# Tile 0 as up 0, up 1, down 0, down 1 with the weights loaded in that order, mixing-weight transposes earlier, batch 1 a group sooner

## Chip, core and metric

The kernel runs on one core of one Trainium2 chip. The metric is device time in microseconds (us) of the whole kernel. A comparison is made of runs on the same chip in the same rounds.

## The reference, cut to what matters

```python
# q, k, v: 8 batches, 8 heads, 576 positions, 64 dims; 4608 = 8 * 576 tokens
scores = scale * q @ k.T                      # per batch and head
ret    = (scores * decay_mask) @ v            # gamma_h ** (i - j) for i >= j, else 0
x      = ret as [4608 tokens, 512]
p      = domain_probs / (domain_probs.sum(-1) + 1e-9)
for e in range(4):                            # w1[e]: 512 x 1024, w2[e]: 1024 x 512
    out += p[:, e] * (relu(x @ w1[e]) @ w2[e])
```

The attention of a batch has to be ready before the expert layers can use its 576 tokens. The expert layers work on nine tiles of 512 tokens.

## The kernel before

TensorE runs the expert layers nearly without a break. The attention of the next batch is threaded between their groups of matmuls. A stage "up e" is 8 groups of 4 matmuls (0.86 us each); a stage "down e" is 4 groups of 8 matmuls (1.73 us each). `plan` says behind which group a piece of attention is issued, so `at(20, ...)` is a place in TensorE's order. 576 is not a multiple of 128: each batch has a remainder of 64 tokens, which is loaded, cast and transposed apart (`load_rem`, `cast_rem`, `Trem`; `Srem` makes its scores and `Orem` its output). Names in the profile: `ph` and `po` are the results of an up and a down group, `ptr` the transposed remainder, `sr` its scores, `s` the scores of other chunks, `qrb`, `krb`, `vrb` the cast remainder and `xT` the attention output that the expert layers read. A load "lands" when it is complete.

```python
def load_rem(b, gate=None):                 # raw_kr, raw_qr, raw_vr on the SP queue
    for n, src in SRC:
        ...
        i = nc.sync.dma_start(out=state[b][n + "r"], in_=src[b, :, SM:S, :].rearrange("h p d -> p h d"))
        if gate is not None and n == "k":
            after(i, gate)                  # SP waits here until the DMA `gate` has landed
...
def moe(nt, lead=0):                        # one tile; every yield ends a group
    ...
    for e in range(E):
        ...                                 # up e: 8 groups, then down e: 4 groups
...
w20 = load_w2(0)                            # weights: POOL queue, in this order
late_constants()
for e in range(1, E):
    load_w1(e)
    load_w2(e)
load_rem(0, w20)                            # the gate: w2 of expert 0
load_alloc(1)
load_chunk(1, 0)
load_chunk(1, 1)
...
if nt == 0:
    at(1, mixing_weights)
    at(3, lambda: a0.cast_rem(nc.gpsimd))   # POOL: krb, qrb, vrb
    at(20, a0.Trem)                         # TensorE: ptr <- qrb, krb
    at(22, a0.Srem, a0.Srem_mask)
    at(24, a0.Orem)
    ...                                     # begin1 at 25: casts of batch 1
elif nt + 1 < B:
    ...
    at(19 if nt == 1 else 17, lambda: state["A"].S([0, 1]))   # scores of the next batch,
                                            # from DMA transposes into qkT
```

Of the kernel before, what the change touches and what calls it, by code (L numbers as in the profile page):

```python
# [9 lines left out]
FP32 = mybir.dt.float32  # L10
BF16 = mybir.dt.bfloat16
# [9 lines left out]
def kernel(  # L21
# [10 lines left out]
    nc = tc.nc  # L32
    B, H, S, D = q.shape
    N, E = moe_domain_probs.shape
    _, Dm, F = moe_w1.shape
# [8 lines left out]
    NFC = F // 128  # L44
    NT = 512
# [108 lines left out]
                   allow_small_or_imprecise_dtypes=True)  # L154
    ident = const.tile([128, 128], BF16)
    make_identity(nc, ident)

    tri2 = const.tile([128, 2, 128], BF16)
    nc.gpsimd.memset(tri2, 1.0)
# [1 line left out]
        nc.gpsimd.affine_select(out=tri2[j:j + 64], in_=tri2[j:j + 64], compare_op=mybir.AluOpType.is_ge,  # L161
                                fill=0.0, base=0, channel_multiplier=-2, pattern=[[-1, 2], [1, 128]])
    tri = const.tile([128, 128], BF16)
    identf = const.tile([NTT, NTT], FP32)


    trir = const.tile([128, R], BF16)
# [1 line left out]
    def late_constants():  # L169
        nc.gpsimd.memset(tri, 1.0)  # L170
        nc.gpsimd.memset(trir, 1.0)
        for j in (0, 64):
            nc.gpsimd.affine_select(out=trir[j:j + 64], in_=trir[j:j + 64], compare_op=mybir.AluOpType.is_ge,
                                    fill=0.0, base=0, channel_multiplier=-1, pattern=[[1, R]])
        nc.gpsimd.affine_select(out=tri, in_=tri, compare_op=mybir.AluOpType.is_ge, fill=0.0,
                                base=0, channel_multiplier=-1, pattern=[[1, 128]])
        nc.gpsimd.tensor_copy(identf, ident[:NTT, :NTT])

    lgp = const.tile([128, NP], FP32)
    for p in range(NP):  # L180
# [19 lines left out]
    probs = const.tile([128, E, NTT], FP32)  # L200
    psm = const.tile([128, NTT], FP32)

    def mixing_weights():
        pp = ps_at.tile([128, E, NTT], FP32, tag="at", name="pp")
        for e in range(E):
            nc.tensor.transpose(pp[:, e, :], probs_raw[:, :, e], identf)
        nc.vector.tensor_copy(probs, pp)
        nc.vector.tensor_reduce(psm, probs[:, :, :].rearrange("p e t -> p t e"),
                                axis=mybir.AxisListType.X, op=ADD)
        nc.vector.tensor_scalar_add(psm, psm, 1e-9)  # L210
        nc.vector.reciprocal(psm, psm)
        nc.vector.tensor_tensor(probs, probs, psm[:, :].unsqueeze(1).to_broadcast([128, E, NTT]), op=MULT)
# [293 lines left out]
                                        gq[:, 2 * u:2 * u + 2, ts], op=MULT)  # L506


    def moe(nt, lead=0):
        n0 = nt * NT  # L510

        def up(ph, e, fc, ts):
            for dc in range(NDC):
                nc.tensor.matmul(ph[:, ts], lhsT=w1_sb[e][:, dc, fc * 128:(fc + 1) * 128],  # L514
                                 rhs=xT[:, dc, n0 + ts.start:n0 + ts.stop], start=(dc == 0), stop=(dc == NDC - 1))

        acc = [apool.tile([128, Dm], FP32, tag="acc", name="acc") for _ in range(NSUB)]
        for e in range(E):
            hT = hpool.tile([128, NFC, NT], BF16, tag="hT")
            for fc in range(NFC):  # L520
                if e == 0 and fc < lead:
                    if fc == 0:
                        early = [ps_mm.tile([128, NT], FP32, tag="mm", name="ph") for _ in range(lead)]
                        for x in range(lead):
                            up(early[x], e, x, slice(0, NT // 2))
                            if x != 1:
                                yield
                    ph = early[fc]
                    up(ph, e, fc, slice(NT // 2, NT))
                else:  # L530
                    ph = ps_mm.tile([128, NT], FP32, tag="mm", name="ph")
                    up(ph, e, fc, slice(0, NT))
                nc.scalar.activation(hT[:, fc, :], ph, Relu)  # L533
                yield
            for ns in range(NSUB):
                t = nt * NSUB + ns
                pe = probs[:, e, t:t + 1]
                last = t == NTT - 1 and e == E - 1
                w = Dm // 2 if last else Dm
                for d in range(0, Dm, w):  # L540
                    po = ps_mm.tile([128, w], FP32, tag="mm", name="po")
                    for fc in range(NFC):
                        nc.tensor.matmul(po, lhsT=hT[:, fc, ns * 128:(ns + 1) * 128],  # L543
                                         rhs=w2_sb[e][:, fc, d:d + w], start=(fc == 0), stop=(fc == NFC - 1))
                    a = acc[ns][:, d:d + w]
                    if e == 0:
                        nc.scalar.activation(a, po, Copy, scale=pe)  # L547
                    else:
                        nc.vector.scalar_tensor_tensor(a, po, pe, a, op0=MULT, op1=ADD)  # L549
                    if e == E - 1:  # L550
                        eng = nc.scalar if last and d // w % 2 else nc.sync
                        eng.dma_start(out=out[n0 + ns * 128:n0 + (ns + 1) * 128, d:d + w], in_=a)
                yield


    a0 = AttP(0)
    UNITS = [(hf, u) for hf in range(2) for u in range(2)]

    tiles = [moe(nt, lead=3 if nt < 2 else 0) for nt in range(n_nt)]
    tile0 = tiles[0]  # L560
    warm(8)
    for n, eng in (("k", nc.gpsimd), ("q", nc.scalar), ("v", nc.gpsimd)):
# [1 line left out]
    for x, (hf, u) in enumerate(UNITS):  # L564
        a0.T(hf, u, nc.scalar)
        if x < 2:
            load_gq((2 + x,))
        if x == 0:
            warm(4)
        else:  # L570
            a0.O(*UNITS[x - 1])
        if x < 3:
            a0.cast("k", *UNITS[x + 1], nc.gpsimd)
            a0.cast("q", *UNITS[x + 1], nc.gpsimd)
            if x:
                load_w1(0, x - 1)
            a0.cast("v", *UNITS[x + 1], nc.gpsimd)
        a0.S(hf, u)
        if x == 0:
            warm(2)  # L580
        a0.kv(hf, u)
    next(tile0)
    a0.O(*UNITS[3])
    next(tile0)
    w20 = load_w2(0)
    late_constants()
    for e in range(1, E):
        load_w1(e)
        load_w2(e)
    load_rem(0, w20)  # L590
# [5 lines left out]
    for nt in range(n_nt):  # L596
        plan = {}

        def at(g, *fs):
            plan.setdefault(g, []).extend(fs)  # L600

        if nt == 0:
            at(1, mixing_weights)
            at(3, lambda: a0.cast_rem(nc.gpsimd))
            at(20, a0.Trem)
            at(22, a0.Srem, a0.Srem_mask)
            at(24, a0.Orem)
            def begin1():
                A = state["a1"] = Att(1)
                for c in range(NCH):  # L610
                    for n in "kqv":
                        A.cast(n, c, nc.gpsimd)
                    if c == 0:
                        load_chunk(1, 2)
                        load_chunk(1, 3)
                load_rem(1)
                load(2)

            at(25, begin1)
            for c, g in enumerate((40, 42, 44, 46)):  # L620
                at(g, lambda c=c: state["a1"].Tc(c))
                if c < 3:
                    at(g + 1, lambda c=c: state["a1"].Sc(c))
                if c > 0:
                    at(g + 1, lambda c=c: state["a1"].Oc(c - 1))
                at(g + 1, lambda c=c: state["a1"].kv(c))
        elif nt + 1 < B:
            if nt == 1:
                a1 = state["a1"]
                at(0, lambda: a1.cast_rem(nc.gpsimd))  # L630
                at(2, a1.Trem)
                at(4, a1.Srem, a1.Srem_mask)
                at(6, a1.Orem)
            def begin(b=nt + 1):
                A = state["A"] = Att(b)
                for c in range(NCH):
                    for n in "kqv":
                        A.cast(n, c, nc.gpsimd)
                A.cast_rem(nc.gpsimd)
                for c in range(NCH + 1):  # L640
                    A.dmaT(c)
                if b + 1 < B:
                    load(b + 1)

            at(7 if nt == 1 else 0, begin)
            at(19 if nt == 1 else 17, lambda: state["A"].S([0, 1]))
            at(24, lambda: state["A"].Srem(), lambda: state["A"].O_values([0, 1]),
               lambda: state["A"].kv_all(), lambda: state["A"].kv_sum(), lambda: state["A"].Srem_mask())
            at(28, lambda: state["A"].O_states([0, 1]))
            at(30, lambda: state["A"].S([2, 3]))  # L650
            at(34, lambda: state["A"].O_values([2, 3], rem=True), lambda: state["A"].O_states([2, 3], rem=True))
        for g, _ in enumerate(tiles[nt]):
            for f in plan.get(g, ()):
                f()
        if nt == 0:
            state["a1"].Sc(3)
            next(tiles[1])
            next(tiles[1])
            state["a1"].Oc(3)


# [28 lines left out]
```

## Time and profile before

| | before |
|---|---|
| median time | 560.77 us (3 runs, before the change was run) |
| TensorE busy | 545.6 of 559.2 us |
| TensorE waits for w2 of expert 0 | 1.74 us, ends at 27.99 |
| gate of the remainder loads opens | 27.96 |
| cast qrb starts / transposes ptr start | 40.99 / 43.64 |

The page of the kernel before, its first parts (busy time and share of the span; granted TensorE clock in tenths per fortieth of the span):

```profile
PE 545.6 (98%) x3469; PEld 262.5 (47%) x3530; DVE 165.7 (30%) x283; ACT 217.0 (39%) x371; POOL 109.8 (20%) x182
PEclk9999999999999999999999999999999999999999
```

TensorE is the bound, at a mean granted clock of 1.000. Only its idle time can be won. The waits of TensorE in the kernel before, one of 0.5 us left out (total us, times, longest us):

```profile
PE pt L437 <- POOL qm L427: 2.3, 3, 1.0
PE po L543 <- DMA wt_492<-in_moe_w_dram: 1.7, 1, 1.7
PE warm_out L140 <- DVE warm_in L135: 1.3, 1, 1.3
PE ph L514 <- DVE xT L329: 0.8, 1, 0.8
...
PE ph L514 <- issue: 0.2, 1, 0.2
```

`wt_492` is w2 of expert 0. About 7 us of idle time in all, of which the change aims at the second, fourth and last line. The weights landed in the order in which they were issued: w2 of expert 0 at 27.95, then w1 and w2 of expert 1 at about 33.0 and 39.6 and w1 of expert 2 at about 45.3 (start of the issue plus time to landing). The SP queue's own waits show the gate:

```profile
SPq L115 <- DMA wt_492<-in_moe_w_dram: 17.0, 1, 17.0
```

TensorE's timeline around the remainder transposes (start, duration, what), and POOL's casts of the remainder:

```profile
41.82 1.89 PE L543 MATMUL po<-wt_502,hT 128*128 128x512 bf16 x8
43.64 0.29 PE L261 MATMUL ptr<-ident,qrb 64*128 64x64 bf16 x4
43.77 0.28 PE L261 MATMUL ptr<-ident,krb 64*128 64x64 bf16 x4
43.98 3.63 PE L543 MATMUL po<-wt_502,hT 128*128 128x512 bf16 x15
47.53 0.31 PE L336 MATMUL sr<-qkT 64*64 64x64 bf16 x8
```

```profile
36.57 1.04 POOL L240 TENSOR_TENSOR krb<-raw_kr,gk 64x512 bf16<-64x512 f32 x1 [13.16 <-DMA raw_kr<-in_k_dram]
40.99 0.60 POOL L243 CAST qrb<-raw_qr 64x512 bf16<-64x512 f32 x1 [3.38 <-DMA raw_qr<-in_q_dram]
```

The cast qrb ends at 41.59 and TensorE asks for it at 43.64: a margin of 2.0 us. The loads of kr and qr took 8.5 and 12.2 us from issue to landing, where the median of all batches is 5.4 and 4.5, because the weight queue was busy. In the half microsecond from 36.0 (weights in 2 KB rows) and in the one from 40.0 (4 KB rows), the two queues moved (packets, MB, share of 16 engines; q0 carries the weights, q1 the SP loads):

```profile
q0 software_dynamic: 78, 0.08, 93.5%
q1 hardware_dynamic: 78, 0.02, 29.9%
```

```profile
q0 software_dynamic: 46, 0.09, 98.9%
q1 hardware_dynamic: 47, 0.01, 18.0%
```

Equal packet counts, so the remainder, in packets of 256 bytes, gets a fifth of the bytes or less. (A weight row of 2 KB is cast to half its size on the way; the trace counts the 1 KB that is written: 0.08 MB in 78 packets.) This fits the round-robin between queue rows of the Trainium skill, "DMA: Bandwidth & Descriptors", section "Queues, rings and completion order". The trace agrees in the equal shares; how many rows an engine takes in one turn it does not show.

### The profile page before, as it was taken

Reading aid. Unit: us, or ns where it says so; the run is one execution under the profiler, and the core shown is the slowest. Engines: PE = TensorE matmul, PEld = TensorE weight load, DVE = VectorE, ACT = ScalarE, POOL = GpSimd, SP = SyncE. Lnnn points to the kernel's source line nnn. Section 1 sums busy time; section 2 is a strip of 40 time slices with the busy share of each in tenths; the row PEclk is TensorE's granted clock in tenths of the full one; section 3 lists DMA queues with packets and bytes.
Section 4 is the critical chain, followed back from the end, with each engine's and each line's share of the span. In section 5 each row is a group of like instructions: output and inputs, shape, how many; then the busy total and the mean of one; then the engine's idle time right before and its main releaser. Section 6 shows DMA issues by size and latency. Waiting matters only on the chain.

```text
span 559.2 us, 8453 instructions
## 1 busy us (share of the span) xinstructions
PE 545.6 (98%) x3469; PEld 262.5 (47%) x3530; DVE 165.7 (30%) x283; ACT 217.0 (39%) x371; POOL 109.8 (20%) x182
## 2 busy tenths in 40 slices
PE   7899999999999999999999999999999999999997
PEld 4544455454445444444445444544444444444443
DVE  5402262253214520462035212542046202220222
ACT  6442344433353235323433334323532353335332
POOL 7611247026001520044002600250010000000000
PEclk9999999999999999999999999999999999999999
DMA  9999999591369025910594058803300100010001
GB/s 232 176 203 200 209 206 231 104 213 15 104 131 180 1 84 89 217 28 38 109 179 92 0 123 157 135 1 98 63 2 1 73 3 0 1 76 0 1 0 75
DMA packets 148277, 53.83 MB, mean 96 GB/s; under 512 B 130668, under 2 KB 142188, under 8 KB 148240
## 3 DMA queue, kind: packets, MB, share of 16 engines
q1 hardware_dynamic: 141296, 44.79, 39.2%
q0 software_dynamic: 6800, 8.39, 8.8%
q8 instruction: 27, 0.44, 0.4%
q10 hardware_dynamic: 144, 0.13, 0.1%
q14 instruction: 10, 0.08, 0.1%
HBM read 45.16 MB, written 9.44 MB: 98 GB/s over the span
## 4 chain that ended last, share of the span: by engine, by line
PE 94%; DMA 3%; POOL 1%; issue 1%; SPq 1%; DVE 0%
PE po L543 44%; PE ph L514 43%; DMA wt_492<-in_moe_w_dram 2%; PE o L351 1%; DMA raw_k<-in_k_dram 1%; PE o L365 1%; SPq L85 1%; POOL km L423 0%; PE sr L336 0%; PE orem L358 0%; PE ptc L297 0%; POOL wt_269 L125 0%; PE kvb L389 0%; PE kva L389 0%; PE oc L322 0%
## 5 line engine op out<-in xcount | busy, mean ns | idle before, releaser
L533 ACT ACTIVATE hT<-ph 128x512 bf16<-128x512 f32 x288 | 171.6, 597 | 274.6 <-PE ph L514 274.6
L543 PEld LDWEIGHTS <-hT 128*128 128x128 bf16 x1160 | 112.5, 98 | 134.6 <-DMA wt_492<-in_moe_w_dram 2.2
L549 DVE SCALAR_TENSOR_TENSOR acc<-po,probs,acc 128x512 f32<-128x512 f32 (+1 forms) x109 | 81.3, 746 | 234.6 <-PE po L543 226.8
L514 PE MATMUL ph<-xT,wt_504 128*128 128x512 bf16 x280 | 66.3, 379 | 0.5
L514 PE MATMUL ph<-xT,wt_269 128*128 128x512 bf16 (+1 forms) x303 | 64.2, 362 | 1.4 <-DVE xT L329 0.8
L543 PE MATMUL po<-wt_492,hT 128*128 128x512 bf16 x286 | 63.4, 379 | 1.8 <-DMA wt_492<-in_moe_w_dram 1.7
L543 PE MATMUL po<-wt_506,hT 128*128 128x512 bf16 x273 | 63.8, 379 | 0.8
L514 PE MATMUL ph<-xT,wt_500 128*128 128x512 bf16 x280 | 64.1, 379 | 0.5
L543 PE MATMUL po<-wt_510,hT 128*128 128x512 bf16 (+1 forms) x287 | 63.4, 373 | 0.5
L514 PE MATMUL ph<-xT,wt_508 128*128 128x512 bf16 x286 | 63.7, 379 | 0.2 <-issue 0.2
L543 PE MATMUL po<-wt_502,hT 128*128 128x512 bf16 x280 | 63.4, 379 | 0.4
L403 POOL CAST sbd<-ksum 64x256 bf16<-64x256 f32 x36 | 14.4, 399 | 221.2 <-DVE ksum L408 197.6
L514 PEld LDWEIGHTS <-wt_269 128*128 128x128 bf16 x312 | 30.0, 98 | 32.1 <-issue 0.9
L514 PEld LDWEIGHTS <-wt_508 128*128 128x128 bf16 x288 | 28.0, 98 | 33.3
L514 PEld LDWEIGHTS <-wt_500 128*128 128x128 bf16 x288 | 27.7, 98 | 33.4
L514 PEld LDWEIGHTS <-wt_504 128*128 128x128 bf16 x288 | 26.9, 98 | 30.3
L547 ACT ACTIVATE acc<-po,probs 128x512 f32<-128x512 f32 x36 | 24.7, 687 | 40.1 <-PE po L543 39.1
L235 POOL TENSOR_TENSOR km<-raw_k,gk 128x512 bf16<-128x512 f32 x28 | 29.2, 1043 | 13.9 <-DMA raw_k<-in_k_dram 9.5
L237 POOL CAST vm<-raw_v 128x512 bf16<-128x512 f32 x28 | 17.3, 616 | 41.8 <-PE o L351 34.9
L237 POOL CAST qm<-raw_q 128x512 bf16<-128x512 f32 x28 | 17.1, 611 | 7.4 <-DMA raw_q<-in_q_dram 7.2
L374 DVE TENSOR_TENSOR xT<-o,gq 128x512 bf16<-128x512 f32 x24 | 15.5, 686 | 7.6 <-PE o L365 7.6
L240 POOL TENSOR_TENSOR krb<-raw_kr,gk 64x512 bf16<-64x512 f32 x8 | 8.3, 1037 | 13.8 <-DMA raw_kr<-in_k_dram 13.2
(231 smaller groups left out, 238.7 us busy)
## 6 DMA issues: line engine op xcount, KB each, us to landing
out_dram<-acc SPq DMA_DIRECT2D x35, 256.0 KB, 2.0
raw_k<-in_k_dram SPq DMA_DIRECT2D x32, 256.0 KB, 5.0
raw_q<-in_q_dram SPq DMA_DIRECT2D x32, 256.0 KB, 5.1
raw_v<-in_v_dram SPq DMA_DIRECT2D x32, 256.0 KB, 5.2
wt_269<-in_moe_w_dram POOLq DMA_DIRECT2D x2, 512.0 KB, 5.6
wt_492<-in_moe_w_dram POOLq DMA_DIRECT2D x1, 1024.0 KB, 11.7
wt_500<-in_moe_w_dram POOLq DMA_DIRECT2D x1, 1024.0 KB, 14.5
wt_502<-in_moe_w_dram POOLq DMA_DIRECT2D x1, 1024.0 KB, 20.4
```

What stands on the lines that cost most here:

```text
L85: nc.sync.dma_start(out=pairs_of(state[b][n, hf])[:, h], in_=src[b, h, 256 * hf:256 * hf + 256, :].rearrange("h (p j) d -> p h (j d)", j=2))
L235: eng.tensor_tensor(o, i, gk[:, c, :].unsqueeze(2).to_broadcast([128, H, D]), op=MULT)
L237: eng.tensor_copy(o, i)
L240: eng.tensor_tensor(self.r["k"], self.t["kr"], gk[:R, NCH, :].unsqueeze(2).to_broadcast([R, H, D]), op=MULT)
L351: nc.tensor.matmul(o[64 * j:64 * j + 64, c * C:(c + 1) * C], lhsT=self.m["v"][:, c, 2 * p + j, :], rhs=self.sT[p][:, j, c, :], start=(c == ...
L374: nc.vector.tensor_tensor(xT[:, p, b * S:b * S + SM], o, gq[:, p, 0:SM], op=MULT)
L403: eng.tensor_copy(sbd[r, n, :, r], src[r])
L514: nc.tensor.matmul(ph[:, ts], lhsT=w1_sb[e][:, dc, fc * 128:(fc + 1) * 128], rhs=xT[:, dc, n0 + ts.start:n0 + ts.stop], start=(dc == 0), s ...
L533: nc.scalar.activation(hT[:, fc, :], ph, Relu)
L543: nc.tensor.matmul(po, lhsT=hT[:, fc, ns * 128:(ns + 1) * 128], rhs=w2_sb[e][:, fc, d:d + w], start=(fc == 0), stop=(fc == NFC - 1))
L547: nc.scalar.activation(a, po, Copy, scale=pe)
L549: nc.vector.scalar_tensor_tensor(a, po, pe, a, op0=MULT, op1=ADD)
```

## The change

The intent: put two up stages ahead of the first down stage, so that w2 of expert 0 is needed one stage (6.9 us) later and its wait goes; fill another wait with the mixing-weight transposes; and have batch 1 ready a group sooner, so that tile 1 does not wait for xT.

```diff
+        first = [ups(0), ups(1), downs(0), downs(1)] if nt == 0 else [ups(0), downs(0), ups(1), downs(1)]
+        for stage in first + [g for e in range(2, E) for g in (ups(e), downs(e))]:
+            yield from stage
...
-    tiles = [moe(nt, lead=3 if nt < 2 else 0) for nt in range(n_nt)]
+    tiles = [moe(0, lead=3, pause=True), moe(1, lead=2, cut=3 * NT // 4)] + [moe(nt) for nt in range(2, n_nt)]
...
+    transposed_probs()
     next(tile0)
     a0.O(*UNITS[3])
     next(tile0)
+    load_w1(1, 0)
+    load_w1(1, 1)
+    late_constants()
     w20 = load_w2(0)
-    late_constants()
-    for e in range(1, E):
+    load_w2(1)
+    for e in range(2, E):
         load_w1(e)
         load_w2(e)
     load_rem(0, w20)
...
-            for c, g in enumerate((40, 42, 44, 46)):
+            for c, g in enumerate((39, 41, 43, 45)):
                 at(g, lambda c=c: state["a1"].Tc(c))
-                if c < 3:
-                    at(g + 1, lambda c=c: state["a1"].Sc(c))
+                at(g + 1, lambda c=c: state["a1"].Sc(c))
...
+            at(47, lambda: state["a1"].Oc(3))
...
-        if nt == 0:
-            state["a1"].Sc(3)
-            next(tiles[1])
-            next(tiles[1])
-            state["a1"].Oc(3)
```

(`moe` split into `ups` and `downs`, and the small constant `identf` made early.) `lead` is how many of a tile's first up groups start on a part of the columns, `cut` how many columns that is: tile 1 starts with 2 x 384 columns in place of 3 x 256. w1 of expert 1 is now loaded in two halves.

More of the change, by code (lines that the diff above doesn't have):

```diff
@@ L156 @@
     make_identity(nc, ident)
+    identf = const.tile([NTT, NTT], FP32)
+    nc.gpsimd.tensor_copy(identf, ident[:NTT, :NTT])
     tri2 = const.tile([128, 2, 128], BF16)
@@ L163 @@
     tri = const.tile([128, 128], BF16)
-    identf = const.tile([NTT, NTT], FP32)
     trir = const.tile([128, R], BF16)
@@ L176, in late_constants @@
                                 base=0, channel_multiplier=-1, pattern=[[1, 128]])
-        nc.gpsimd.tensor_copy(identf, ident[:NTT, :NTT])
     lgp = const.tile([128, NP], FP32)
@@ L201, with transposed_probs @@
     psm = const.tile([128, NTT], FP32)
-    def mixing_weights():
-        pp = ps_at.tile([128, E, NTT], FP32, tag="at", name="pp")
+    def transposed_probs():
+        pp = ps_mm.tile([128, E, NTT], FP32, tag="mm", name="pp")
         for e in range(E):
@@ L207, in mixing_weights @@
         nc.vector.tensor_copy(probs, pp)
+    def mixing_weights():
         nc.vector.tensor_reduce(psm, probs[:, :, :].rearrange("p e t -> p t e"),
@@ L506, in O, with moe @@
                                         gq[:, 2 * u:2 * u + 2, ts], op=MULT)
-    def moe(nt, lead=0):
+    def moe(nt, lead=0, cut=NT // 2, pause=False):
         n0 = nt * NT
@@ L517, in moe, with ups @@
         acc = [apool.tile([128, Dm], FP32, tag="acc", name="acc") for _ in range(NSUB)]
-        for e in range(E):
-            hT = hpool.tile([128, NFC, NT], BF16, tag="hT")
-            for fc in range(NFC):
-                if e == 0 and fc < lead:
-                    if fc == 0:
-                        early = [ps_mm.tile([128, NT], FP32, tag="mm", name="ph") for _ in range(lead)]
-                        for x in range(lead):
-                            up(early[x], e, x, slice(0, NT // 2))
-                            if x != 1:
-                                yield
+        hTs = {}
+        def ups(e):
+            hT = hTs[e] = hpool.tile([128, NFC, NT], BF16, tag="hT", name="hT")
+            n = lead if e == 0 else 0
+            early = [ps_mm.tile([128, NT], FP32, tag="mm", name="ph") for _ in range(n)]
+            for x in range(n):
+                up(early[x], e, x, slice(0, cut))
+                if pause and x != 1:
+                    yield
+            for fc in range(NFC):
+                if fc < n:
                     ph = early[fc]
-                    up(ph, e, fc, slice(NT // 2, NT))
+                    up(ph, e, fc, slice(cut, NT))
                 else:
@@ L534, in moe, with downs @@
                 yield
+        def downs(e):
+            hT = hTs[e]
             for ns in range(NSUB):
```

## The prediction

> **What bounds the kernel.** TensorE: busy 545.6 of 559.2 us (98%, the page) at granted clock 1.0, and 94% of the chain of waits. The PE view of the waits lists about 7 us of idle time, all in the first 87 us. What the change can touch: 1.74 us at 26.25 for the first down weights (w2 of expert 0, landed 27.95), 0.78 us at 86 for xT of batch 1's last chunk, 0.3 us at 17.2 for w1 of expert 0, 0.16 us of issue at 70. About 3 us (0.5%) is the most it can win.
>
> **What it changes.** No arithmetic is added or removed.
> 1. Tile 0 runs up 0, up 1, down 0, down 1. w2 of expert 0 is needed 6.9 us later (one stage), but both halves of w1 of expert 1 go ahead of it. The weight queue is first in, first out; at its packet rate per window (163 per us of 2 KB rows), w1 of expert 1 lands at 23.5 and 26.6 (needed 26 and 29.3), w2 of expert 0 at about 33.6 (needed 32.7). The 1.74 us wait becomes 0 to 1 us.
> 2. The four mixing-weight transposes (0.67 us) fill the 0.3 us wait for w1: 0.3 to 0.4 us.
> 3. Batch 1 a group sooner, and tile 1 starting with 2x384 columns: removes the 0.78 us wait, the 0.16 us, and about 0.1 us of narrow matmuls (24 of 256 columns, 118 ns each, become 20, mostly wider). About 1.0 us.
>
> **What it delays, unmentioned.** The remainder loads of batch 0 (kr, qr, vr) are gated on the landing of w2 of expert 0: SP's queue view shows the wait, 17.0 us, ended at 27.96. The gate now opens about 5.6 us later. Before, these loads crawled: first packets 4 us after issue, kr landed 36.5, qr 40.9, vr about 45.7. In every half microsecond both queues moved equal packet counts (80 and 78 beside 2 KB weight rows, 46 and 45 beside 4 KB rows). That agrees with the Trainium skill, "DMA: Bandwidth & Descriptors", section "Queues, rings and completion order": each DMA engine goes round-robin between queue rows by packet. Same counts shifted: qr lands 46 to 47.5, its POOL cast ends 47 to 48. The remainder transposes stay at the same group (TensorE there at 43.64 before, about 42.4 after). Margin before: 2.0 us. After: a TensorE stall of about 4.5 us, so that point moves from 43.64 to about 47.2, +3.5 us. vr (about 51) is needed about 54: no wait. Chunks of batch 1 come 1 to 2 us later, TensorE later still: no new wait.
>
> **Sum.** +3.5 - 1.0 = +2.5 us: 563.2 us; range 560.0 to 565.2. Chances: faster by over 2% 0.005, within 2% 0.985, slower 0.01. Without the stall about 557.8.
>
> **What would show it.** The PE wait for w2 of expert 0 at most 1 us; a new wait of the remainder transposes (ptr) for the POOL cast qrb, 3 to 6 us, near 42; SP's gate opening near 33.5; no wait for xT at the start of tile 1; after 90 us a constant shift of about +2.5 us.
>
> **What would make it wrong.** kr and qr moving sooner after the gate (first packets after 2.5 us instead of 4) or beside 2 KB rows for longer cuts the stall by 1 to 2 us. w2 landing late adds nothing by itself, since the later stall absorbs it, but moves the gate. If batch 1's casts became the limit at group 39, a wait for qm or vm would appear there.

## The result, and the profile after

A ratio here is taken by the benchmark from the fast runs of both kernels in the same rounds, so it is not quite the ratio of the medians beside it. The medians are 565.35 us after (564.40 to 566.02, 6 runs) and 560.93 us before (6 runs); the ratio is 1.0077, 95% interval 1.0064 to 1.0091: about 4.3 us slower. The prediction was 563.2 with a range up to 565.2.

The profiled run took 566.02 us, the slowest of the six. Its page:

```profile
PE 552.0 (98%) x3526; PEld 263.5 (47%) x3526; DVE 165.7 (29%) x283; ACT 216.8 (38%) x371; POOL 110.4 (20%) x183
PEclk9997999999999999999999999999999999999999
```

The 7 is new: in the fourth slice (42 to 56 us) the granted clock was not full. The three longest waits of TensorE and the SP gate after:

```profile
PE ptr L263 <- POOL qrb L245: 5.2, 1, 5.2
PE warm_out L140 <- DVE warm_in L135: 1.3, 1, 1.3
PE pt L439 <- POOL qm L429: 1.3, 1, 1.3
```

```profile
SPq L115 <- DMA wt_507<-in_moe_w_dram: 21.6, 1, 21.6
```

The wait for w2 (now `wt_507`) and the wait for xT are gone, as intended. The gate opens at 33.09 instead of 27.96, and one large wait has come: ptr for qrb. TensorE's timeline and POOL's casts in the same place after:

```profile
40.34 1.89 PE L550 MATMUL po<-wt_509,hT 128*128 128x512 bf16 x8
47.47 0.39 PE L263 MATMUL ptr<-ident,qrb 64*128 64x64 bf16 x4 [5.24 <-POOL qrb L245]
47.68 0.40 PE L263 MATMUL ptr<-ident,krb 64*128 64x64 bf16 x4
48.01 5.74 PE L550 MATMUL po<-wt_509,hT 128*128 128x512 bf16 x16
53.68 0.31 PE L338 MATMUL sr<-qkT 64*64 64x64 bf16 x8
```

```profile
43.30 1.04 POOL L242 TENSOR_TENSOR krb<-raw_kr,gk 64x512 bf16<-64x512 f32 x1 [18.59 <-DMA raw_kr<-in_k_dram]
46.81 0.60 POOL L245 CAST qrb<-raw_qr 64x512 bf16<-64x512 f32 x1 [2.48 <-DMA raw_qr<-in_q_dram]
```

ptr starts 3.83 us later than before (47.47 against 43.64). But two groups on, sr starts 6.15 us later (53.68 against 47.53). The same down groups between them took 5.74 us instead of 3.63. Windows of TensorE, every second microsecond (window, its length, busy us, instructions, granted clock, DMA share, GB/s), say why:

```profile
41.00:42.00 1.00, 1.00 (x6) 1.00 1.15 210
43.00:44.00 1.00, 0.00 (x0) 1.00 1.20 196
45.00:46.00 1.00, 0.00 (x0) 0.74 1.20 194
47.00:48.00 1.00, 0.53 (x8) 0.50 1.21 194
49.00:50.00 1.00, 1.00 (x4) 0.50 1.10 194
51.00:52.00 1.00, 1.00 (x4) 0.50 1.13 211
53.00:54.00 1.00, 1.00 (x13) 1.00 1.16 210
```

The clock was halved from about 45.5 to 52.3, while TensorE still waited and on for 4.8 us after it had work again. PE reads as fully busy there, but a window counts 4 matmuls (those cut by its edges included) where one at full clock counts 6. After that the shift stays near 6.15 us until the end of tile 0 and is 5.16 us at the first down stage of tile 1 (98.80 against 93.64): the third part of the change won its 1.0 us.

So the profiled pair adds up as +3.83 (stall, net of the w2 wait won) + 2.32 (half clock) - 0.99 (batch 1 sooner) = +5.16 us, against 564.3 - 559.2 = 5.1 us of span. The other five runs are shorter by about 0.9 us on average. The profiled run had one more half-clock stretch, from 11.4 to 14.8 us, in the loading phase; its mean granted clock was 0.991, that of the others 0.993 to 0.994. I estimate from these means that each of the others was at half clock for 7 to 8 us, about as long as the stretch behind the stall.

A second profile of the same stall: after_s21 below is the changed kernel up to 100 us. There the gate opened at 31.73 and the split is another one:

```profile
46.44 0.39 PE L263 MATMUL ptr<-ident,qrb 64*128 64x64 bf16 x4 [5.38 <-POOL qrb L245]
53.20 0.31 PE L338 MATMUL sr<-qkT 64*64 64x64 bf16 x8
```

ptr is 2.80 us later than before and sr 5.67 us, so the stall costs 2.80 us and the half clock (45.6 to 52.4) 2.87 us, in which the profile has a pause of 0.2 us as well.

### The profile page after: what moved, and what is told of

Same layout as the page of the kernel before. It is cut to its first block, busy times and chain, and to the rows that moved or that the text cites. A ratio compares the mean times of both kernels' runs of the same rounds, so it can differ in the third digit from the quotient of the medians.

```text
span 564.3 us, 8505 instructions
## 1 busy us (share of the span) xinstructions
PE 552.0 (98%) x3526; PEld 263.5 (47%) x3526; DVE 165.7 (29%) x283; ACT 216.8 (38%) x371; POOL 110.4 (20%) x183
## 4 chain that ended last, share of the span: by engine, by line
PE 91%; DMA 6%; POOL 2%; SPq 1%; issue 0%; DVE 0%
PE po L550 43%; PE ph L516 42%; DMA wt_507<-in_moe_w_dram 2%; DMA raw_qr<-in_q_dram 2%; PE o L353 1%; DMA raw_k<-in_k_dram 1%; PE o L367 1%; SPq L85 1%; POOL km L425 0%; PE sr L338 0%; PE orem L360 0%; PE ptc L299 0%; POOL wt_270 L125 0%; PE kvb L391 0%; PE kva L391 0%; POOL wt_499 L125 0%
## 5 line engine op out<-in xcount | busy, mean ns | idle before, releaser
L550 PE MATMUL po<-wt_509,hT 128*128 128x512 bf16 x288 | 66.1, 388 | 0.0
L550 PE MATMUL po<-wt_513,hT 128*128 128x512 bf16 x288 | 64.6, 379 | 0.0
L516 PE MATMUL ph<-xT,wt_270 128*128 128x512 bf16 (+3 forms) x308 | 64.4, 365 | 0.0
L550 PE MATMUL po<-wt_507,hT 128*128 128x512 bf16 x288 | 63.6, 379 | 0.0
```

Source lines behind the costliest of these rows:

```text
L516: nc.tensor.matmul(ph[:, ts], lhsT=w1_sb[e][:, dc, fc * 128:(fc + 1) * 128], rhs=xT[:, dc, n0 + ts.start:n0 + ts.stop], start=(dc == 0), s ...
L550: nc.tensor.matmul(po, lhsT=hT[:, fc, ns * 128:(ns + 1) * 128], rhs=w2_sb[e][:, fc, d:d + w], start=(fc == 0), stop=(fc == NFC - 1))
```

## The experiments

Twelve kernels were run. The table sums them up; "before" is the median of the kernel before in the same rounds.

| run | median us | before us | ratio (95%) |
|---|---|---|---|
| gate_w1 | 561.14 | 560.87 | 1.0007 (0.9989 to 1.0025) |
| fill_stall | 564.17 | 560.87 | 1.0054 (1.0042 to 1.0066) |
| order_alone | 566.84 | 560.87 | 1.0102 (1.0089 to 1.0116) |
| batch1_alone | 561.15 | 560.87 | 1.0005 (0.9993 to 1.0017) |
| gate_w1_s21 | 559.09 | 561.01 | 0.9960 (0.9949 to 0.9972) |
| trem_24_s21 | 557.92 | 561.01 | 0.9945 (0.9932 to 0.9958) |
| gate_late_in_before | 566.43 | 561.01 | 1.0093 (1.0077 to 1.0110) |
| batch1_s21 | 559.74 | 561.01 | 0.9974 (0.9962 to 0.9986) |
| trem_22_s21 | 561.13 | 561.14 | 0.9997 (0.9971 to 1.0024) |
| trem_21_s21 | 563.88 | 561.14 | 1.0049 (1.0028 to 1.0070) |
| after_s21 | 565.16 | 561.14 | 1.0071 (1.0048 to 1.0093) |
| before_s21 | 560.71 | 561.14 | 0.9986 (0.9960 to 1.0011) |

The theory at the outset: the later gate makes the remainder late, TensorE stalls for it, and the idle time makes the clock fall. The rivals: the new stage order or the weight loads cut in halves cost by themselves; or the slow stretch behind the stall has another cause.

### gate_w1: the gate alone, in the changed kernel

```diff
-    load_w1(1, 1)
+    w11 = load_w1(1, 1)
-    load_rem(0, w20)
+    load_rem(0, w11)
```

> The changed kernel with one edit: the remainder loads of batch 0 are gated on the second half of w1 of expert 1 (landing near 27) and not on w2 of expert 0 (33.1). Theory (late gate, stall, clock drop): the wait of ptr for qrb (5.2 us) and the half-clock stretch behind it vanish together; 557.5 to 558.5 us, 2.5 to 3.5 us faster than before. Rival (the new stage order or the halved weight loads cost by themselves): above 560.5 us although the wait is gone.

Measured: 561.14 us, 4.2 us better than the changed kernel's median, but no better than before. They were run at other times. By the number the rival was met (above 560.5 us). The wait for qrb is gone (ptr at 41.84), yet the expected gain is not there. The TensorE waits and the timeline of the profiled run, the slowest of the six (563.56 us), show where it went:

```profile
PE s L278 <- DMA qkT<-km: 2.3, 1, 2.3
```

```profile
105.95 0.45 PE L278 MATMUL s<-qkT 64*128 64x128 bf16 x6
108.73 0.45 PE L278 MATMUL s<-qkT 64*128 64x128 bf16 x10 [2.34 <-DMA qkT<-km]
```

At the first scores of batch 2 TensorE waits for DMA transposes. The last that it needs was issued at 106.17. In the kernel before, that transpose and the scores stand here:

```profile
105.04 1.26 SPq L268 DMA_TRANSPOSE qkT<-km  x1
107.55 0.23 PE L276 MATMUL s_1438<-qkT 64*128 64x128 bf16 x1
```

With the median of 2.5 us from issue to landing, I estimate that it lands in the kernel before at about 107.5; TensorE was there at 107.55. So before was balanced on this point without a wait: a second wall, made by the SP and POOL chain of batch 2's loads, casts and transposes, 60 us behind the first. What tile 0 saves beyond that is given back there. The wall is not a fixed time: here the chain itself ran 1.1 us later than before although TensorE came earlier, and why is not shown. In this profile the clock then fell to half from 109.6 to 113.0 as well; in four of the six runs the mean clock was 0.999 or 1.0, and these took 559.94 to 561.94 us. Both the theory (of the stall) and the rival were thus incomplete: the wait for qrb went, the gain did not come, and the new order was not the reason (gate_w1_s21 and trem_24_s21 below keep it and are faster).

### fill_stall: TensorE kept busy in the stall

```diff
-            at(20, a0.Trem)
+            at(20, lambda: warm(23), a0.Trem)    # 23 dummy matmuls 128x512
```

> The changed kernel with 23 dummy matmuls (about 4.9 us at full clock) just ahead of the remainder transposes, so that the 5.2 us stall stays but TensorE is not idle in it. Theory (a clock drop after the idle time costs about 2.3 us over and above the stall): ptr still starts near 47.5, granted clock 1.0 throughout, 562.5 to 563.5 us. Rival (the slow stretch at 48 to 53 us comes from DMA traffic or PSUM, not from idleness): the slow matmuls stay and the time is 565 us or more.

Measured: 564.17 us, about 0.5 us above the expected range. The timeline of this kernel:

```profile
41.27 5.13 PE L140 MATMUL warm_out<-warm_in 128*128 128x512 bf16 x23
47.41 0.29 PE L263 MATMUL ptr<-ident,qrb 64*128 64x64 bf16 x4 [1.01 <-POOL qrb L245]
47.53 0.28 PE L263 MATMUL ptr<-ident,krb 64*128 64x64 bf16 x4
47.74 3.63 PE L550 MATMUL po<-wt,hT 128*128 128x512 bf16 x16
51.30 0.31 PE L338 MATMUL sr<-qkT 64*64 64x64 bf16 x8
```

ptr starts at the same time as in the changed kernel (47.41 against 47.47), but the 16 down matmuls take 3.63 us instead of 5.74 and sr starts at 51.30 instead of 53.68. The granted clock is 0.999 to 1.0 in all five runs. The DMA issues are the same, and from 42 to 54 us both profiles have the same traffic (201 GB/s, DMA share 1.18), so it is the idleness that slows the stretch, not the traffic. The profiles put the clock at 2.4 us; the ratios of the two kernels to before (1.0077 and 1.0054) put it at 0.0023 times 561 us, 1.3 us. The dummy work costs nothing, because TensorE had nothing to do.

### order_alone: the new order of stages and weights alone

The parts "transposes" and "batch 1" of the change are undone, the order stays.

```diff
-    tiles = [moe(0, lead=3, pause=True), moe(1, lead=2, cut=3 * NT // 4)] + [moe(nt) for nt in range(2, n_nt)]
+    tiles = [moe(0, lead=3, pause=True), moe(1, lead=3, pause=True)] + [moe(nt) for nt in range(2, n_nt)]
-    transposed_probs()
...                                   # batch 1 at groups 40, 42, 44, 46 again
```

> Before plus the new order of stages and weights alone (transposes and batch 1 as before). Theory: the whole loss sits here: wait for w2 gone (-1.7), stall of ptr and half clock (+5 and +2.3): 566 to 567 us. Rival (the loss comes from batch 1 a group sooner or the moved transposes): at or under 561 us.

Measured: 566.84 us. The whole loss sits in this part, and it is larger than that of the full change (ratio 1.0102 against 1.0077), which fits the 1.0 us that batch 1 wins. The wait for qrb is 4.3 us here: in this profile TensorE reached ptr 0.6 us later (42.8 against 42.2). The prediction's 0.3 to 0.4 us for moving the mixing-weight transposes was not measured alone; in the full change an earlier TensorE only waits longer for qrb. In this profile the clock fell only at 48.2, 1.1 us after TensorE had work again, and for 3.4 us.

### batch1_alone: batch 1 a group sooner alone

```diff
-        first = [ups(0), ups(1), downs(0), downs(1)] if nt == 0 else [ups(0), downs(0), ups(1), downs(1)]
+        first = [ups(0), downs(0), ups(1), downs(1)]
...                                   # weights in the order of before, transposes as before
```

> Before plus batch 1 a group sooner and the 2x384 start of tile 1, nothing else. Theory: -1.0 us, 559.7 to 560.3 us, the 0.78 us wait for xT gone. Rival (the casts of batch 1, which land between 62 and 75 us, make TensorE wait when asked a group sooner without the delay of the full change): a wait of ptc or kvp for qm or vm, and no gain.

Measured: 561.15 us, no gain: the theory's number missed. The wait for xT is gone, but the wait that the rival named (casts of batch 1) did not come. Instead the second wall shows again:

```profile
PE s L276 <- DMA qkT<-km: 1.3, 1, 1.3
```

### gate_w1_s21: the early gate, and the scores of batch 2 later

```diff
-            at(19 if nt == 1 else 17, lambda: state["A"].S([0, 1]))
+            at(21 if nt == 1 else 17, lambda: state["A"].S([0, 1]))
```

on top of gate_w1.

> gate_w1 with one more edit: in tile 1 the first scores of batch 2 (S) come two groups (3.46 us) later. gate_w1 itself gave no gain (561.1): its profile shows TensorE there at 106.4 waiting 2.3 us for the DMA transposes of batch 2, then about 3.8 us at half clock. Theory (a second wall: batch 2's transposes land near 107 to 109 whatever tile 0 does, so what tile 0 saves is given back there): the wait is gone and the time is 557.5 to 559.0 us. Rival (the new order costs something else that the wait merely hides): no better than 560.5.

Measured: 559.09 us, 0.4% faster than before and just past the top of the expected range. The wait for qkT is gone and the clock is 1.0. One wait of 1.0 us for the cast qm of batch 1 (ptc, at 72.80) has appeared, as TensorE now comes to batch 1's third chunk earlier than its data. (The 3.8 us at half clock in the expectation are 3.4 us in the trace of gate_w1, 109.6 to 113.0.)

### trem_24_s21: the late gate kept, TensorE asks later

```diff
-            at(20, a0.Trem)
+            at(24, a0.Trem)
-            at(22, a0.Srem, a0.Srem_mask)
+            at(26, a0.Srem, a0.Srem_mask)
-            at(24, a0.Orem)
+            at(28, a0.Orem)
-            at(25, begin1)
+            at(29, begin1)
```

and the scores of batch 2 at 21.

> The changed kernel with its late gate kept, but the remainder transposes four groups later (24 instead of 20, scores 26, output 28, batch 1's casts from 29) and S of batch 2 two groups later. DMA order and gate are those of the changed kernel, only TensorE asks later. Theory (the loss is the stall of TensorE on qrb and its clock drop, not slower loads): no wait for qrb over 0.5 us, granted clock 1.0, 557.5 to 559.5 us. Rival (the late gate costs by delaying all later loads): above 560.5 us, with waits of ptc or kvp for batch 1's casts or of s for qkT.

Measured: 557.92 us, ratio 0.9945: the best version, 3.1 us faster than before. Here the gate opens about as late as in the other kernels with the new order and the late gate (31.74; the others 31.73 to 33.09) and qrb is cast as late (46.26; the others 45.78 to 47.02). It costs nothing, because TensorE comes to ptr with other work done, and does not wait:

```profile
47.38 0.29 PE L263 MATMUL ptr<-ident,qrb 64*128 64x64 bf16 x4
```

All of TensorE's waits in this kernel:

```profile
PE pt L439 <- POOL qm L429: 1.7, 3, 0.8
PE warm_out L140 <- DVE warm_in L135: 1.3, 1, 1.3
PE pt L439 <- ACT qm L427: 0.6, 1, 0.6
```

Only the loading phase is left.

### gate_late_in_before: the late gate alone, in the kernel before

```diff
-        load_w1(e)
+        g = load_w1(e)
         load_w2(e)
-    load_rem(0, w20)
+        if e == 1:
+            w11 = g
+    load_rem(0, w11)
```

> The kernel before with one edit: the remainder loads wait for w1 of expert 1 (landing near 33.0) and not for w2 of expert 0 (27.95), all else as before. Theory (the gate's time alone makes the loss): ptr waits 3 to 4.5 us for qrb, granted clock at half for some us behind it, 565 to 567 us; the w2 wait of 1.7 us stays. Rival (the gate needs the new stage order to hurt): within 1 us of before.

Measured: 566.43 us, in the expected range. The gate opens at 32.60 and ptr waits:

```profile
PE ptr L261 <- POOL qrb L243: 3.8, 1, 3.8
PE pt L437 <- POOL qm L427: 1.9, 3, 0.8
PE po L543 <- DMA wt<-in_moe_w_dram: 1.6, 1, 1.6
```

Neither the new stage order nor the halved loads are needed for the loss: the later gate makes it by itself. The six runs fall into two kinds by mean granted clock: three at 0.997 (565.05, 564.90 and 566.08 us) and three at 0.993 or 0.994 (567.26, 567.78 and 566.79 us), on average 1.9 us apart. I estimate from these means a half-clock stretch of about 3.4 us in the one kind and 7 to 8 us in the other (the profiled run, of the second kind, has 6.8). So the same program pays for the clock differently from run to run.

### batch1_s21: batch 1 sooner, with the second wall moved

batch1_alone with the scores of batch 2 at 21 instead of 19.

> batch1_alone with S of batch 2 two groups later. batch1_alone gave 561.15 against 560.87: it removed the 0.78 us wait for xT and showed a new wait of 1.3 us for batch 2's transposes. Theory (second wall): with S later the gain comes through, 559.5 to 560.2 us. Rival (batch 1 a group sooner gains nothing by itself): 560.7 or more.

Measured: 559.74 us, ratio 0.9974, by which it is 1.5 us faster than before, inside the expected range. The wait for qkT is gone: the gain comes through once the second wall is out of the way.

### after_s21 and before_s21: the controls

The changed kernel and the kernel before, each with only the scores of batch 2 at 21.

> The changed kernel with S of batch 2 two groups later and nothing else. Theory: its stall puts TensorE behind batch 2's transposes already, so S later gains nothing: 564.5 to 566.0 us, like the changed kernel. Rival (S two groups later is itself worth 1 us or more): 564 or less.

> The kernel before with S of batch 2 two groups later. In its profile S did not wait for the transposes. Theory: same as before within 0.5 us (560.5 to 561.5). Rival (S later is worth something by itself, so the gains of gate_w1_s21 and batch1_s21 are not the change's): 560 or less.

Measured: 565.16 us, like the changed kernel; and 560.71 us with an interval that holds 1 (0.9960 to 1.0011). So moving the scores is no gain in itself that can be told from noise. That it lets other gains through rests on the profiles, where the wait for qkT is there without it and gone with it. The times alone do not settle it for the smaller gains: the interval of before_s21 reaches down to 0.9960, as far as the ratio of gate_w1_s21 and further than that of batch1_s21.

### trem_22_s21 and trem_21_s21: a shorter stall

As trem_24_s21, with the remainder transposes at group 22 (scores 24, output 26, casts from 27) and at group 21 (23, 25, 26).

> As trem_24_s21 (557.9 us, no stall) but the remainder transposes only two groups later than in the changed kernel (22). TensorE reaches them 3.46 us later than there, so about 1.5 to 2 us of the 5.2 us stall are left. Theory (the stall adds itself, and the clock falls only after an idle stretch well above 2 us): 559.3 to 560.3 us, granted clock 1.0. If the clock falls after such a short wait too: 560.5 to 562 us with a half-clock stretch.

> Remainder transposes one group later than in the changed kernel (21): a stall of about 3.3 to 3.7 us is left. Theory (stall 3.5 us plus one window of half clock, 3.4 us long, which costs about 1.7 us): 562.5 to 563.7 us with a half-clock stretch in the profile. If the clock stays: 561.2 to 561.8.

Measured at 22: 561.13 us, but in two kinds: 559.93 and 560.22 us at a clock of 0.999 and 1.0, 562.05 and 562.19 us at 0.997 and 0.996. The profiled run is the one of 559.93, with a stall of 2.1 us and full clock. The two slower ones were not profiled, so that their clock fell behind this stall is inferred from the means. By that, with a stall of this size it is chance whether the clock falls. The expectation that it would not was wrong for half of the runs. Measured at 21: 563.88 us, a little over the range; the profile has a stall of 4.6 us, longer than I expected, and half clock from 46.2 to 53.0, twice as long as I expected. The time falls step by step with the stall, with the DMA order unchanged: 565.16 (after_s21), 563.88, 561.13 and 557.92 us for stalls of 5.4, 4.6, 2.1 and 0 us in the profiles.

## Why the prediction was wrong

- What bounds the kernel, and the ceiling of about 3 us: right. The best version wins 3.1 us.
- The wait for w2 of expert 0 goes: right (0 to 1 us predicted, none measured). The gate opens near 33.5: 33.09. A new wait of ptr for qrb, about 4.5 us: 5.2. ptr at about 47.2: 47.47. No wait for xT, and batch 1's part worth 1.0 us: 0.99 in the profiled pair. The direction and the mechanism of the loss were right, and gate_late_in_before shows the gate making it alone.
- The step that failed is the sum, "+3.5 - 1.0 = +2.5 us", and with it "after 90 us a constant shift of about +2.5 us". It counted a stall of 4.5 us as 4.5 us of lost time and left out the term for what the stall does to TensorE's clock. That term was put at nothing. It measured 2.3 us in the profiled pair, 2.4 against fill_stall and 2.9 in the profile of after_s21; by the rounds of fill_stall it is 1.3 us. The term for the stall was near: +3.8 and, in after_s21, +2.8, for +3.5. Without the clock term, fill_stall at 564.17 us lies inside the range; with it the result lies 0.15 us outside.
- The Trainium skill states this. "TensorE: Matmul & The Clock Gate", section "Part 1: The HAM clock gate (the "warmup" mystery)", says that after an idle window of about 3.4 us the array's clock is halved and comes back after a busy window, and that the windows run free of the kernel, so that the cost differs from run to run. Its section "Why this matters for your kernels" says: "No PE-idle gaps >~3µs between matmul bursts". The prediction put down a gap of 4.5 us and says nothing of the clock. The traces agree with the windows: half clock for 6.8 us (two windows) here, in after_s21, trem_21_s21 and gate_late_in_before, for 3.4 us (one) in gate_w1 and order_alone, and two kinds of runs of gate_late_in_before. The clock fell 2.8 us after TensorE went idle in gate_late_in_before, 3.3 us after here, 4.5 us after in after_s21 and 5.3 us after in order_alone.
- "Without the stall about 557.8" was wrong for the change as it stands. gate_w1 took the stall away and gave 561.14 us, because of batch 2's transposes at 107 us. The step that failed is the assumption that a microsecond saved in tile 0 stays saved: the prediction's "no new wait" looks at the chunks of batch 1 and does not go on to batch 2. With that wall moved the number comes near: 559.09 us in gate_w1_s21, where a wait of 1.0 us for qm is left, and 557.92 us in trem_24_s21, where none is.

Open: what the moved mixing-weight transposes are worth alone; how stall and clock split in the unprofiled runs of the changed kernel, where the two profiles have 3.8 + 2.3 and 2.8 + 2.9 us and the rounds of fill_stall give 1.3 us for the clock; and what moves batch 2's chain by a microsecond from kernel to kernel.

## What to carry to other kernels

When weights are reordered, look for every load and wait that is gated on one of them: the gate moves along, and what hangs on it may have less margin than the thing that was improved. When a wait of 2 us or more lands on TensorE, allow for its clock (here about 2 us brought it down in some runs and not in others, and 3.8 to 5.4 us in every profile in which TensorE stood idle for that long), or fill the wait with dummy matmuls, which were free here. Before counting a saving, walk on along the data chains of the next stages: a chain that was just in time before, such as the transposes at 107.5 us, will give the saving back.

## What the Trainium skill lacked or had wrong

- "TensorE: Matmul & The Clock Gate" advises, in "Why this matters for your kernels", against idle gaps over about 3 us. Here the clock fell after a single shorter one: in gate_w1 TensorE was idle for 2.34 us (106.4 to 108.7) and was at half clock from 109.6 to 113.0, after work had begun again. The matmuls just ahead of and behind the gap were small ones (64x128), so low activity around it may have counted, which no run here tells apart. With a planned stall near 2 us (trem_22_s21) the mean clock was 0.996 and 0.997 in two of four runs, which were not profiled.
- The same page says that the count of slow matmuls differs from run to run, but gives the cost of a gap only for a kernel that waits at every step of its loop. For one gap in a busy kernel it was one or two windows of half clock here: in gate_late_in_before the six runs split into two kinds 1.9 us apart, with mean clock 0.997 and 0.993 to 0.994. Nor does it say that dummy matmuls put into a gap keep the clock up: fill_stall stayed at 0.999 to 1.0.
- "DMA: Bandwidth & Descriptors" gives a fixed cost of about 2 us for a DMA (fitted on the GpSimd queue) and about 0.6 us to the first byte on the SP queue. No page gives a figure for the first packet beside a queue that is busy: in the kernel before the first remainder packets moved about 3.9 us after the issue at 27.96, and about 4 us after the issue at 33.09 in the changed kernel. That the busy queue causes this delay is not shown.
